# Making the 64-wide triangular inverses of chunks 0 to 11 from 16-wide blocks on VectorE and four products on TensorE

## The chip, the core and the metric

The kernel runs on one core of one Trainium2 chip. The metric is the device time of one execution in microseconds; a core has five engines that run side by side, each with its own queue in order: TensorE (PE; PEld are its weight loads), VectorE (DVE), ScalarE (ACT), GpSimd (POOL) and SyncE (SP), which here issues nearly all DMAs.

## What is computed

For 4 batches of 8 heads, 768 time steps and a head width of 40, a linear recurrence carries a 40x40 state; its outputs go through a gated network with a spatial mixing over time. Cut to what matters (all float32):

```python
for t in range(S):                       # S = 768, state [B, H, D, D], D = 40
    y[:, :, t] = einsum('bhd,bhde->bhe', r_t, state)
    Sa = einsum('bhde,bhe->bhd', state, a_t)
    state = state * w_t[:, :, None, :] - einsum('bhd,bhe->bhde', Sa, b_t) \
          + einsum('bhd,bhe->bhde', v_t, k_t)
x = y as [B, S, H * D]                   # H * D = 320
h = maximum(x @ w_in, 0)                 # d_ff = 1024
u, v = h[..., :512], h[..., 512:]
v_n = (v - mean(v)) / sqrt(var(v) + 1e-6)
out = (u * (einsum('ts,bsd->btd', w_spatial, v_n) + b_spatial[:, None])) @ w_out
```

## The kernel before

Time is cut into chunks of 64 steps. Two batches go together, so there are 24 chunks (`NS`), 12 for each pair of batches, and each chunk has 16 units (2 batches x 8 heads): 8 places in the free dimension (`NU`) times two halves of the partitions (0 to 63 and 64 to 127; `par` in the code).

Within a chunk the recurrence is turned into matrix products. The dependence of a step on the steps before it is a strictly lower triangular 64x64 matrix L for each unit, and the inverse of (1 + L), transposed, is needed as the tile `xf`. A chunk runs through these steps, each named as in the code:

- **Preparation** (`prep_load`, `prep_piece`, `scan1`, `scan2`, `at_mul`, `sl_mul`): VectorE scans the decays and multiplies the keys with them. It runs four or more chunks ahead. `lprime` and `lblock` make the two 32x32 diagonal blocks of each unit's L and put them, masked with `maskl`, into `Lc`, in which four chunks (a group, `GS`) come together.
- **Inversion** (`invert`): VectorE transposes a group's `Lc` so that every partition holds one 32x32 block, runs 30 pairs of multiply (into the PSUM tile `itmp`) and add (into `A`) over growing and shrinking rectangles, and transposes the result back twice, once straight (`XT0`) and once transposed (`X11`). Group 0 is inverted in one go before chunk 0; the steps of the others are spread between the work of earlier chunks.
- **Assembly** of the 64-wide inverse: `b_l21` multiplies out the off-diagonal 32x32 block, `b_zt` and `b_x21` multiply it with the two diagonal inverses on TensorE; ScalarE evicts (`b_l21_out`, `b_zt_out`, `b_x21_out`) and copies the diagonal blocks into `xf` (`b_xcopy`).
- **Other work ahead of the chain:** `b_copy` (a DMA into `At`), `b_lka` and `b_h` (products that ScalarE evicts and GpSimd's `strict` masks), `b_tok` (transposes).
- **The chain from chunk to chunk:** `c_bp` (products with the state `Mc`), `c_ff`, `c_xx` (products with `xf`), `c_mp` and `c_mp_out` (the new `Mc`), `c_y` and `c_y_out` (the outputs, a multiply on VectorE, line 654), `y_store`.
- **The dense network** from chunk 11 on, between the chunks: `m_load`, `m_split`, `m_u`, `m_v`, `m_n1` to `m_n3`. Its weights are decoded on VectorE and ScalarE (`decode64_steps`) during chunks 4 to 9. The spatial mixing and the last product follow in `phase2`.

The order of all this is written out by hand. `at(t, fn, ...)` puts a step into a plan at the time t, counted in chunks ("slot 3" is t from 3 to 4); the plan is sorted and issued in that order, so it sets every engine's queue. The times in a chunk's slot come from dictionaries:

```python
REG = dict(copy=0.11, lka=0.115, lka_out=0.17, tok=0.40, ..., x=0.50, x21=0.78, x21_out=0.81, dt=0.03)
LEAD = dict(REG, zt=0.88, zt_out=0.90, x=0.975, x21=1.12, x21_out=1.16)
```

The assembly for chunk q stands in slot q-1 (`REG`); that of a group's first chunk reaches into slot q (`LEAD`), as does that of chunk 1 (`FIRST`). All the small products before the chain (`lprime`, `b_lka`, `b_tok`, `b_h` and the assembly) share the two PSUM buffers named `bk`.

Of the kernel before, what the change touches and what calls it, by code (L numbers as in the profile page):

```python
# [217 lines left out]
def phase1(ctx, tc, early, late, vtok, win, xs, vns, uts, dscr):  # L218
# [125 lines left out]
    def lblock(s):  # L344
        if s % GS == 0:
            st["Lc", s // GS] = inv.tile([P, GS * NU, HB], F32, name="Lc")
        Lc = st["Lc", s // GS]
# [1 line left out]
        nc.vector.tensor_tensor(
            out=Lc[:, u0:u0 + NU, :], in0=st.pop(("pl", s)),  # L350
            in1=maskl.unsqueeze(1).broadcast_to([P, NU, HB]), op=ALU.mult,
        )

    def invert(g):
        Lc = st.pop(("Lc", g))
        A = inv.tile([P, HB, HB], F32, name="A")
        nc.vector.transpose(out=A, in_=Lc.rearrange("p u t -> p t u"))
        yield
        nc.vector.memset(A.rearrange("p t s -> p (t s)")[:, 0:HB * HB:HB + 1], 1.0)
        for k in range(1, HB - 1):  # L360
            m = HB - 1 - k
# [1 line left out]
            nc.vector.tensor_tensor(  # L363
                out=tp, in0=A[:, k + 1:, k:k + 1].broadcast_to([P, m, k]),
                in1=A[:, k:k + 1, 0:k].broadcast_to([P, m, k]), op=ALU.mult,
            )
# [5 lines left out]
        nc.vector.transpose(out=XT0.rearrange("p u t -> p t u"), in_=A)  # L372
        yield
        nc.vector.transpose(out=X11.rearrange("p u t -> p t u"), in_=A.rearrange("p t s -> p s t"))
        yield

    INV_N = HB + 1
# [33 lines left out]
    def b_lka_out(s, par):  # L411
# [3 lines left out]
        if s in LKA_POOL:  # L415
            nc.scalar.activation(At[par][ev], pk[ev], AF.Copy)  # L416
# [18 lines left out]
    def b_h_out(s, par):  # L435
        ev = PR[1 - par]
        Rt = Rts[s % 2]
        if s in H_POOL:
            nc.scalar.activation(Rt[par][ev, :, 0:C], st["ph", s][ev], AF.Copy)
# [84 lines left out]


# [60 lines left out]
    def c_xx_out(s, g):  # L586
# [3 lines left out]
        if s in TRI_POOL:  # L590
            for par in range(2):
                done = nc.scalar.activation(Rt[par][PR[par], gp], xx[PR[1 - par]], AF.Copy, scale=-1.0)  # L592
            marks["a", s] = done.ins
            for par in range(2):
                strict(Rt[par][PR[par], gp, 0:C], NP)
            return
        for par in range(2):
            nc.scalar.activation(Rt[par][PR[par], gp, C:], xx[PR[1 - par], :, C:], AF.Copy, scale=-1.0)
        for par in range(2):
            ur, ev = PR[par], PR[1 - par]  # L600
            nc.vector.tensor_tensor(
                out=Rt[par][ur, gp, 0:C], in0=xx[ev, :, 0:C],
                in1=maskn[ev].unsqueeze(1).broadcast_to([64, NP, C]), op=ALU.mult,
            )
# [421 lines left out]
```

## Time and profile before

| | |
|---|---|
| median of 3 runs | 669.57 us (663.91 to 670.55) |
| profiled execution | 665.08 us, span 663.3 us, mean granted clock 0.943 |
| PE busy | 571.8 us (86%) |
| PEld busy | 518.3 us (78%) |
| DVE busy | 448.4 us (68%) |
| ACT busy | 384.2 us (58%) |
| POOL busy | 225.9 us (34%) |

The span is the profiled execution from its first to its last instruction; its time has 1.8 us around that. Busy times are sums over the span, and engines lead in different parts of it. PEclk is the clock that TensorE was granted, as a share of full speed; a product takes longer at a lower one. In rows of instructions "128x30" is partitions x elements, "64\*64 64x104" is the weight tile and the moving tile, and "x32" counts records; one float32 product of these sizes leaves two. Releasers behind "<-" say what an engine waited for.

### The profile page before, as it was taken

The page shows a single profiled execution, that of the slowest core. Times are in us where ns is not written, and L with a number is a line of the kernel's source. Part 1 is how long each engine was busy: PE and PEld are TensorE (multiplying, and loading weights), DVE is VectorE, ACT ScalarE, POOL GpSimd, SP SyncE. Part 2 cuts the span into 40 slices and gives each one's busy share as a digit, 9 for nine tenths or more (in the row PEclk, how much of TensorE's full clock was granted, in tenths as well). Part 3 has the DMA queues.
Part 4 walks back from the last instruction along what each step waited for, and adds up shares of the span by engine and source line. Part 5 has one row for each costly group of instructions (what it writes and reads, how often), then busy time and mean ns, then how long its engine had stood idle before and what let it go on. Part 6 is the DMA issues. An engine that isn't in the chain of part 4 may idle for free.

```text
span 663.3 us, 25848 instructions
## 1 busy us (share of the span) xinstructions
PE 571.8 (86%) x10960; PEld 518.3 (78%) x10960; DVE 448.4 (68%) x970; ACT 384.2 (58%) x860; POOL 225.9 (34%) x298
## 2 busy tenths in 40 slices
PE   1447885498777887999999999999989999999997
PEld 1437674487766776888888888888878999999997
DVE  8999789989999999488896677343384842332220
ACT  2135662377666775688878887888765543221212
POOL 6013330224332334144341332332354843352221
PEclk9967997789787898999999999999998999999999
DMA  8654778477555546657565365375395557150001
GB/s 199 121 107 67 134 152 147 70 175 155 135 127 115 131 117 120 142 127 172 154 190 148 86 173 144 90 198 132 89 262 182 162 155 240 61 157 31 31 31 59
DMA packets 106331, 87.68 MB, mean 132 GB/s; under 512 B 35496, under 2 KB 92072, under 8 KB 104296
## 3 DMA queue, kind: packets, MB, share of 16 engines
q1 hardware_dynamic: 105672, 84.31, 52.0%
q10 hardware_dynamic: 544, 1.72, 1.2%
q8 instruction: 86, 1.41, 1.0%
q14 instruction: 29, 0.24, 0.1%
HBM read 59.20 MB, written 20.50 MB: 120 GB/s over the span
## 4 chain that ended last, share of the span: by engine, by line
PE 63%; DVE 15%; DMA 7%; issue 6%; ACT 4%; SPq 3%; POOL 1%; DVEq 0%; ACTq 0%; POOLq 0%
PE po L199 6%; PE pv L759 6%; PE pv L712 6%; PE pg L179 5%; PE pg L180 5%; PE pg L181 5%; PE ch L563 4%; PE bp L545 4%; PE ch L581 4%; PE bk L429 2%; DMA ein<-in_early 2%; DVE itmp L363 2%; PE bk L451 2%; PE bk L399 2%; PE bp L641 2%
## 5 line engine op out<-in xcount | busy, mean ns | idle before, releaser
L406 POOL TENSOR_SCALAR_AFFINE_SELECT Rt<-Rt 64x512 f32<-64x512 f32 (+1 forms) x144 | 83.8, 584 | 156.2 <-ACT Rt L592 128.5
L406 POOL TENSOR_SCALAR_AFFINE_SELECT At<-At 64x512 f32<-64x512 f32 x48 | 41.5, 864 | 164.0 <-ACT At L416 151.9
L555 ACT ACTIVATE Rt<-bp 64x416 f32<-64x416 f32 x96 | 49.1, 511 | 56.2 <-PE bp L545 53.6
L363 DVE TENSOR_TENSOR itmp<-A 128x30 f32<-128x30 f32 (+9 forms) x180 | 66.5, 369 | 3.4
L179 PE MATMUL pg<-wsh,vh 128*128 128x384 f32 x192 | 65.4, 341 | 2.0 <-ACT vh L51 2.0
L545 PE MATMUL bp<-lin,Mc 40*64 40x104 f32 x768 | 47.3, 278 | 22.1 <-DVE y L654 19.8
L183 DVE TENSOR_TENSOR g<-pg,bb 128x384 f32<-128x384 f32 x32 | 17.8, 556 | 70.7 <-PE pg L181 68.4
L180 PE MATMUL pg<-wsl,vh 128*128 128x384 f32 x192 | 65.1, 339 | 0.0
L181 PE MATMUL pg<-wsh,vl 128*128 128x384 f32 x192 | 63.6, 339 | 0.0
L367 DVE TENSOR_TENSOR A<-A,itmp 128x30 f32<-128x30 f32 (+9 forms) x180 | 59.1, 328 | 6.2
L545 PEld LDWEIGHTS bp<-lin,Mc 40*64 40x64 f32 x768 | 40.7, 150 | 25.5 <-DVE y L654 22.7
L563 PE MATMUL ch<-Rt,At 128*64 128x104 f32 x768 | 48.0, 283 | 5.9 <-issue 4.8
L55 POOL TENSOR_TENSOR gl<-g,gh 128x384 fp32r<-128x384 f32 x32 | 33.0, 1035 | 58.1 <-ACT gh L51 58.1
L592 ACT ACTIVATE Rt<-ch 64x416 f32<-64x416 f32 x96 | 49.1, 511 | 4.6 <-PE ch L581 2.2
L563 PEld LDWEIGHTS ch<-Rt,At 128*64 128x64 f32 x768 | 42.2, 157 | 10.4 <-issue 7.1
L51 ACT ACTIVATE gh<-g 128x384 fp32r<-128x384 f32 x32 | 16.7, 521 | 54.3 <-DVE g L184 54.3
L339 PE MATMUL bk<-at,sl 64*32 64x32 f32 x1536 | 21.2, 203 | 26.5 <-DVE sl L324 20.7
L55 POOL TENSOR_TENSOR vl<-raw,vh 128x512 fp32r<-128x512 f32 x24 | 31.5, 1324 | 31.6 <-ACT vh L51 30.1
L581 PE MATMUL ch<-ffs,xf 64*64 64x104 f32 x768 | 41.7, 261 | 0.0
L339 PEld LDWEIGHTS bk<-at,sl 64*32 64x32 f32 x1536 | 17.7, 114 | 29.5 <-issue 14.4
L179 PEld LDWEIGHTS pg<-wsh,vh 128*128 128x128 f32 x192 | 36.6, 190 | 2.4 <-ACT vh L51 2.2
L630 DVE TENSOR_TENSOR Mc<-ch,scn 104x160 f32<-104x160 f32 x44 | 18.5, 436 | 29.0 <-PE ch L619 18.7
(132 smaller groups left out, 1497.8 us busy)
## 6 DMA issues: line engine op xcount, KB each, us to landing
ein<-in_early SPq DMA_DIRECT2D x108, 129.0 KB
lin<-in_late SPq DMA_DIRECT2D x48, 160.0 KB
At<-at SPq DMA_DIRECT2D x48, 128.0 KB
...
```

Of the source, the lines that this page charges most:

```text
L55: eng.tensor_tensor(out=lo, in0=x, in1=hi.bitcast(F32), op=ALU.subtract)
L179: nc.tensor.matmul(pg, lhsT=vh[:, dc], rhs=w_h, start=(i == 0), stop=False)
L180: nc.tensor.matmul(pg, lhsT=vh[:, dc], rhs=w_l, start=False, stop=False)
L181: nc.tensor.matmul(pg, lhsT=vl[:, dc], rhs=w_h, start=False, stop=(i == NT - 1))
L363: nc.vector.tensor_tensor(out=tp, in0=A[:, k + 1:, k:k + 1].broadcast_to([P, m, k]), in1=A[:, k:k + 1, 0:k].broadcast_to([P, m, k]), op=AL ...
L367: nc.vector.tensor_tensor(out=A[:, k + 1:, 0:k], in0=A[:, k + 1:, 0:k], in1=tp, op=ALU.add)
L406: nc.gpsimd.affine_select(out=t, in_=t, pattern=[[0, k], [1, C]], base=0, channel_multiplier=-1, compare_op=ALU.is_gt, fill=0.0,)
L545: nc.tensor.matmul(bp[PR[par], q, :], lhsT=Mc[RR[par], n, :], rhs=li[RR[par], n, C:], start=(q == 0), stop=False, skip_group_check=True,)
L555: nc.scalar.activation(Rt[par][PR[par], gp, :], st["bp", g][PR[par]], AF.Copy)
L563: nc.tensor.matmul(ff[PR[1 - par], q, :], lhsT=At[par][:, n, :], rhs=Rt[par][:, n, :], start=True, stop=True,)
L581: nc.tensor.matmul(xx[ev, q, :], lhsT=xf[ev, n, :], rhs=ffs[ev, q, :], start=True, stop=True,)
L592: done = nc.scalar.activation(Rt[par][PR[par], gp], xx[PR[1 - par]], AF.Copy, scale=-1.0)
```

## The change

For groups 0, 1 and 2 (`INV16`), that is chunks 0 to 11, VectorE inverts only the four 16x16 diagonal blocks of each unit, two at a time in one instruction, in 14 pairs of steps instead of 30. The mask `maskl` gets a second version that keeps the 16-wide blocks. X11 comes before XT0 in these groups.

TensorE then makes the 64-wide inverse. With D the block-diagonal inverse and N the part of L outside the 16-wide blocks, `b_no` multiplies out L and `b_no_out` evicts the columns outside the blocks in three ScalarE instructions with a mask column of `cm` as scale (into `noT`); `b_diag` spreads the inverted blocks over a 64-wide tile, twice (D and its transpose), by two multiplies on GpSimd each (on ScalarE for the first D of chunk 0); `b_k1` multiplies N with D and ScalarE evicts K1; `b_y1`, `b_y2` and `b_y3` multiply K1 with what is there, the first and the third result are added to `xf` on VectorE, the second is evicted by ScalarE. Each of these products is 64x64x64 for each of the 16 units. They take the place of `b_l21`, `b_zt` and `b_x21`; groups 3, 4 and 5 keep these.

Around it, `maskp` and `maskn` go with the branches that used them (which no chunk took), `l21` and `zt` share buffers with the new tiles, the plan gets new times, the loads and scans of some chunks, the decoding and the first loads and splits of the dense network move by less than half a slot, and every third `vr` of the dense network lies in `noT`.

```diff
+    INV16 = {0, 1, 2}
+    ADD1, ADD3, DACT = (), (), {0}
+    S0 = (0.4, 0.401, 0.402, 0.4005, 0.405, 0.406, 0.41, 0.411, 0.415, 0.416)
+    SREG = {'no': 0.28, 'no_out': 0.285, 'd0': 0.23, 'k1': 0.36, 'k1_out': 0.365, 'd1': 0.24, 'y1': 0.66, 'y1_out': 0.665, 'y2': 0.8, 'y2_out': 0.805, 'y3': 0.98, 'y3_out': 0.985}
+    SLEAD = {'no': 0.44, 'no_out': 0.445, 'd0': 0.88, 'k1': 0.9, 'k1_out': 0.905, 'd1': 0.89, 'y1': 1.02, 'y1_out': 1.025, 'y2': 1.1, 'y2_out': 1.105, 'y3': 1.22, 'y3_out': 1.225}
+    SFIRST = {'no': 0.407, 'no_out': 0.408, 'd0': 0.43, 'k1': 0.85, 'k1_out': 0.855, 'd1': 0.44, 'y1': 1.06, 'y1_out': 1.065, 'y2': 1.12, 'y2_out': 1.125, 'y3': 1.2, 'y3_out': 1.205}
...
     def invert(g):
+        wide = g in INV16
+        W = SB if wide else HB
+        nb = HB // W
...
-        for k in range(1, HB - 1):
-            m = HB - 1 - k
-            tp = ps_i.tile([P, m, k], F32, name="itmp")
+        for k in range(1, W - 1):
+            m = W - 1 - k
+            tp = ps_i.tile([P, nb, m, k], F32, name="itmp")
             nc.vector.tensor_tensor(
-                out=tp, in0=A[:, k + 1:, k:k + 1].broadcast_to([P, m, k]),
-                in1=A[:, k:k + 1, 0:k].broadcast_to([P, m, k]), op=ALU.mult,
+                out=tp, in0=B[:, :, k + 1:W, k:k + 1].broadcast_to([P, nb, m, k]),
+                in1=B[:, :, k:k + 1, 0:k].broadcast_to([P, nb, m, k]), op=ALU.mult,
             )
...
+    def b_no(s):
+        Et, at, sl = st["pre", s]
+        m1 = ps_k.tile([P, NU, C], F32, name="bk")
+        for n in range(NU):
+            for par in range(2):
+                nc.tensor.matmul(
+                    m1[PR[1 - par], n, :], lhsT=sl[PR[par], n, par, :], rhs=at[PR[par], n, :],
+                    start=True, stop=True,
+                )
+    def b_no_out(s):
+        for j in range(1, C // SB):
+            cs = slice(j * SB, (j + 1) * SB)
+            nc.scalar.activation(noT[:, :, cs], m1[:, :, cs], AF.Copy, scale=cm[:, j - 1:j])
+    def b_diag(s, k):
+        out = xfs[s % 2] if k else st["D", s]
+        for h in range(2):
+            dst, src, m = out[:, :, h * HB:(h + 1) * HB], st["X", s // GS][1 - k][:, u0:u0 + NU], cm[:, 3 + h:4 + h]
+            if s in DACT and not k:
+                nc.scalar.activation(dst, src, AF.Copy, scale=m)
+            else:
+                nc.gpsimd.tensor_scalar(out=dst, in0=src, scalar1=m, scalar2=None, op0=ALU.mult)
+    def blocks(s, lhsT, rhs, add=None):
+        ps = ps_k.tile([P, NU, C], F32, name="bk")
+        for n in range(NU):
+            for ev in PR:
+                nc.tensor.matmul(ps[ev, n, :], lhsT=lhsT[ev, n, :], rhs=rhs[ev, n, :], ...)
+        return ps
+    def b_k1(s):      st["ps", s] = blocks(s, noT, st["D", s])
+    def b_k1_out(s):  nc.scalar.activation(k1, st["ps", s], AF.Copy)
+    def b_y1(s):      st["ps", s] = blocks(s, st["K1", s], xf, ...)
+    def b_y2(s):      st["ps", s] = blocks(s, st["K1", s], xfs[s % 2])
+    def b_y2_out(s):  nc.scalar.activation(y2, st["ps", s], AF.Copy)
+    def b_y3(s):      st["ps", s] = blocks(s, st["K1", s], st["D", s], ...)
+    def b_add(s, on_pe):                       # y1_out and y3_out
+        nc.vector.tensor_tensor(out=xf, in0=st["ps", s], in1=xf, op=ALU.add)
...
-    SCR, SLM = {4: 0.68}, {5: 0.83}
-    PREP = {4: 0.03, 5: 0.45, 6: 1.03, 7: 1.45, 8: 2.03, 9: 2.45, 10: 3.03, 11: 3.45}
+    PREP = {4: 0.207, 5: 0.53, 6: 1.03, 7: 1.41, 8: 2.03, 9: 2.45, 10: 2.88, 11: 3.45, 14: 6.05, 12: 3.93}
+    LPQ = {5: 1.15, 6: 0.78, 13: 0.78, 4: 1.05}
+    INV_T = {1: (2.5, 3.7), 2: (4.5, 7.4)}
+    OV = {(scr_store, 4): 0.68, (sl_mul, 5): 1.13, (scan2, 4): 0.4075, (at_mul, 4): 0.497, (sl_mul, 4): 0.507, (scan2, 5): 0.96, (at_mul, 5): 0.97, (scan1, 11): 3.61}
...
-    T_DEC, T_MOE = 4.2, 11
+    T_DEC, DSP, T_MOE = 4.03, 0.953, 11
...
-        at(max(own[0] - 1.6, 2 * j + 2.1, T_DEC + 5.92), m_load, bq, i)
-        at(max(own[0] - 0.45, 2 * j + 2.7), m_split, bq, i)
+        at(max(own[0] - 1.6, 2 * j + 2.1, T_DEC + 5 * DSP + 7 * 0.1 + 0.02), m_load, bq, i)
+        at(max(own[0] - 0.6, 2 * j + 2.7), m_split, bq, i)
```

The twelve times of a series' steps (`no` to `y3_out`) are those of `SREG`, `SLEAD` (first chunks of groups 1 and 2), `SFIRST` (chunk 1) and `S0` (chunk 0).

More of the change, by code (lines that the diff above doesn't have):

```diff
@@ L371, in invert, with inv_n @@
         st["X", g] = (XT0, X11)
[L372 to L377, printed above, removed]
+        outs = [(XT0, A), (X11, A.rearrange("p t s -> p s t"))]
+        for x, a in outs[::-1] if wide else outs:
+            nc.vector.transpose(out=x.rearrange("p u t -> p t u"), in_=a)
+            yield
+    def inv_n(g):
+        return (SB if g in INV16 else HB) + 1
     def lin_load(s, par):
@@ new lines, in blocks @@
+    def blocks(s, lhsT, rhs, add=None):
+        ps = ps_k.tile([P, NU, C], F32, name="bk")
+        if add is not None:
+            nc.tensor.matmul(ps, lhsT=ident, rhs=add, start=True, stop=False, skip_group_check=True)
+        for n in range(NU):
+            for ev in PR:
+                nc.tensor.matmul(
+                    ps[ev, n, :], lhsT=lhsT[ev, n, :], rhs=rhs[ev, n, :], start=add is None, stop=True,
+                    skip_group_check=add is not None,
+                )
+        return ps
@@ L589, in c_xx_out @@
         xx = st["xx", g]
[L590 to L596, printed above, removed]
         for par in range(2):
-            nc.scalar.activation(Rt[par][PR[par], gp, C:], xx[PR[1 - par], :, C:], AF.Copy, scale=-1.0)
+            done = nc.scalar.activation(Rt[par][PR[par], gp], xx[PR[1 - par]], AF.Copy, scale=-1.0)
+        marks["a", s] = done.ins
         for par in range(2):
[L600 to L604, printed above, removed]
+            strict(Rt[par][PR[par], gp, 0:C], NP)
     def c_mp(s, g):
@@ L812, in phase1 @@
         at(T["lka"], b_lka, q)
+        at(T["h"], b_h, q)
+        if q // GS in INV16:
+            S = SFIRST if q == 1 else SREG if q % GS else SLEAD
+            series(q, {k: q - 1 + t for k, t in S.items()})
+            continue
         at(T["l21"], b_l21, q)
@@ L894, in phase1 @@
             p.affine_select(
-                out=maskl[rows], in_=maskl[rows], pattern=[[1, HB]], base=0,
+                out=maskl[rows], in_=maskl[rows], pattern=[[0, 2], [1, HB]], base=0,
                 channel_multiplier=-1, compare_op=ALU.is_gt, fill=0.0,
+            )
+            p.affine_select(
+                out=maskl[rows, 1, SB:], in_=maskl[rows, 1, SB:], pattern=[[0, SB]], base=1 - SB,
+                channel_multiplier=1, compare_op=ALU.is_gt, fill=0.0,
             )
@@ L905, in phase1 @@
         make_identity(nc, ident)
-        for m, val in ((maskp, 1.0), (maskn, -1.0)):
-            p.memset(m, val)
-            for rows in PR:
-                p.affine_select(
-                    out=m[rows], in_=m[rows], pattern=[[1, C]], base=0,
-                    channel_multiplier=-1, compare_op=ALU.is_gt, fill=0.0,
-                )
+        p.memset(cm, 1.0)
+        p.memset(cm[:, 0:3], -1.0)
+        for rows in PR:
+            p.affine_select(
+                out=cm[rows, 0:3], in_=cm[rows, 0:3], pattern=[[SB, 3]], base=SB,
+                channel_multiplier=-1, compare_op=ALU.is_gt, fill=0.0,
+            )
+            p.memset(cm[rows.start:rows.start + HB, 4:5], 0.0)
+            p.memset(cm[rows.start + HB:rows.stop, 3:4], 0.0)
+        p.memset(noT[:, :, 0:SB], 0.0)
         for t in (Mc, *xfs):
@@ L944, in phase1 @@
             b_tok_out(0, par)
[L945 to L946 removed]
+        if 0 in INV16:
+            b_no(0)
+            b_no_out(0)
+        else:
+            b_l21(0)
+            b_l21_out(0)
         b_h(0)
```

143 lines of the change are left out of this document (87 added, 56 removed).

## The prediction

> **What bounds the kernel now.** I began with the page: how the five engines stand and how that changes over the span.
>
> ```profile
> PE 571.8 (86%) x10960; PEld 518.3 (78%) x10960; DVE 448.4 (68%) x970; ACT 384.2 (58%) x860; POOL 225.9 (34%) x298
> ...
> PE   1447885498777887999999999999989999999997
> ...
> DVE  8999789989999999488896677343384842332220
> ```
>
> TensorE (PE) has the most work, but a slice is 16.6 us, and up to the 16th (some 265 us) VectorE (DVE) shows 7 to 9 while PE shows 1 to 9; from there PE stands at 9. So there are two kernels in one: VectorE leads up to chunk 11, TensorE from there to the end, and the edit trades work of the first for work of the second just where the roles change. The trade has to be made stage by stage. The last of a chunk's y multiplies (line 654) marks its end; that of chunk 11 is shown, and I cut the busy time of the engines at the ends of chunks 0, 1, 3, 7, 9 and 11.
>
> ```profile
> 277.38 0.42 DVE L654 TENSOR_TENSOR y<-bp,Et 104x256 f32<-104x256 f32 x1 [0.78 <-PE bp L641]
> core 0: us, PE busy (x) PEld busy (x) DVE busy (x) ACT busy (x) POOL busy (x), PEclk, DMA share, GB/s
> ...
> 26.00:54.10 28.10, 14.09 (x259) 12.84 (x258) 25.95 (x65) 10.57 (x24) 4.17 (x6) 0.67 0.41 77
> 54.10:65.30 11.20, 10.46 (x302) 9.09 (x301) 10.32 (x15) 7.88 (x20) 6.34 (x6) 0.77 0.56 85
> 65.30:82.30 17.00, 14.03 (x443) 12.06 (x431) 12.10 (x17) 11.48 (x27) 6.27 (x9) 1.00 0.78 137
> 82.30:134.20 51.90, 31.66 (x952) 27.79 (x954) 47.88 (x97) 22.55 (x52) 11.90 (x16) 0.84 0.66 121
> 134.20:206.90 72.70, 58.47 (x1680) 51.50 (x1677) 67.87 (x134) 49.99 (x113) 23.77 (x32) 0.90 0.64 143
> 206.90:241.80 34.90, 30.05 (x824) 26.84 (x826) 33.89 (x69) 25.00 (x57) 10.36 (x16) 0.86 0.55 122
> 241.80:277.80 36.00, 30.61 (x743) 27.00 (x740) 26.95 (x53) 23.43 (x53) 12.37 (x18) 0.91 0.64 134
> 277.80:475.10 197.30, 196.12 (x4364) 170.20 (x4353) 127.85 (x333) 161.47 (x367) 67.77 (x104) 1.00 0.53 143
> ```
>
> In the rows from 82.3 to 241.8 VectorE works 149.6 of 159.5 us. In the row from 65.3 to 82.3 it does not lead; there one chunk costs PE 14.0 us at the full granted clock (1.00), the yardstick for a chunk without the edit. In the last row PE is busy 196.1 of 197.3 us: when PE is the bound, this program leaves it hardly any idle time. Nothing of the edit works there, so I carry every microsecond won before 277.8 to the end unchanged.
>
> **The removed work.** The first inversion stands alone on VectorE:
>
> ```profile
> 26.02 1.94 DVE L357 STREAM_TRANSPOSE A<-Lc 128x1024 f32<-128x1024 f32 x1
> 28.03 0.20 DVE L363 TENSOR_TENSOR itmp<-A 128x30 f32<-128x30 f32 x1
> ...
> 30.20 0.40 DVE L363 TENSOR_TENSOR itmp<-A 128x130 f32<-128x130 f32 x1
> ...
> 52.17 1.97 DVE L374 STREAM_TRANSPOSE X<-A 128x1024 f32<-128x1024 f32 x1
> 56.42 3.04 PE L581 MATMUL ch<-ffs,xf 64*64 64x104 f32 x32
> 82.30:134.20 51.90, 25.86 (x64) 0.84 0.66 121
> 134.20:206.90 72.70, 27.68 (x64) 0.90 0.64 143
> ```
>
> (The xx products of chunk 0 start at 56.4; the last two rows count only what touches the tile A: inversions 1 and 2, 25.9 and 27.7 us.) Thirty pairs and three transposes take 26.02 to 54.1, 28.1 us. The 14 new pairs have 28 to 112 elements; four old pairs of 30 to 108 elements take 28.03 to 30.20, 0.54 us each. So 14 x 0.56 = 7.9 us, with three transposes of 1.9 in all 13.6: **about 14 us less per inversion**, 42 us for three. The second block in the access pattern has no row. I bound it by nothing and by 0.1 us an instruction (130 elements took 0.40 once, twice the 0.20 of 30), 2.8 us an inversion, and take nothing: the cost follows the count of elements.
>
> **The added work.** Prices come from the nearest rows:
>
> ```profile
> 67.99 1.15 PE L399 MATMUL bk<-at,sl 64*64 64x64 f32 x32 [0.84 <-ACT Rt L555]
> 69.07 1.65 PE L563 MATMUL ch<-Rt,At 128*64 128x104 f32 x32
> ...
> 80.07 0.69 PE L514 MATMUL bk<-zt,X 32*32 32x32 f32 x32
> 80.69 1.09 PE L641 MATMUL bp<-Rt,tk 128*40 128x64 f32 x32
> L183 DVE TENSOR_TENSOR g<-pg,bb 128x384 f32<-128x384 f32 x32 | 17.8, 556 | 70.7 <-PE pg L181 68.4 <-POOL gl L55 2.3
> L349 DVE TENSOR_TENSOR Lc<-bk,maskl 128x256 f32<-128x256 f32 x24 | 10.1, 419 | 5.5 <-PE bk L339 5.5
> L406 POOL TENSOR_SCALAR_AFFINE_SELECT Rt<-Rt 64x256 f32<-64x256 f32 x96 | 50.0, 521 | 137.2 <-ACT Rt L592 128.5 <-PE ch L581 2.4 <-POOL Rt L406 0.4
> L439 ACT ACTIVATE Rt<-bk 64x512 f32<-64x512 f32 x48 | 28.0, 584 | 2.3 <-PE bk L429 1.6
> L776 ACT ACTIVATE xf<-XT 128x256 f32<-128x256 f32 x24 | 9.9, 413 | 11.6 <-DVE XT L372 11.4
> ```
>
> - **TensorE (PE):** sixteen 64x64 products (32 records) take from 67.99 to the next start at 69.07, 1.08 us; sixteen 32-wide ones 80.07 to 80.69, 0.62. A chunk gets five for three: 5.4 - 1.9 = **+3.5 us**, 42 us over 12 chunks. VectorE's 42 us come back as PE time; the gain is only what PE can take in its gaps.
> - **VectorE:** two adds of 128x512 from PSUM per chunk. By the slope of 0.42 us (256 elements) to 0.56 (384), 0.69 each: **+1.4 us** a chunk.
> - **ScalarE:** nine small copies go, three of 128x128 and two of 128x512 (0.58) come: a little less work on an engine with room.
> - **GpSimd:** four multiplies of 128x256 a chunk have no row; between 0.4 (ScalarE's copy of that size) and twice the 64x256 select, 1.0; I take 0.5, as that select. 2 us a chunk beside 6.3 in a slot of 17: hidden unless rival B holds.
>
> At one place the Trainium skill speaks otherwise. TensorEngine Tiling (Array Packing), section Instruction Overhead, has about 60 cycles for any small matmul, so 32 and 64 columns would cost about the same; the rows above (0.62 against 1.08 us) disagree. By that rule the extra of a chunk would be two products of 0.62, 1.2 us, and the sum that of rival A.
>
> **The sum, stage by stage,** against the profiled execution's own 665.08 us:
>
> 1. Start. Inversion 0 gives X11 at about 37.7 instead of XT at 52.2: -14.5. Then chunk 0's series stands on the path alone: diagonals (0.8 on ScalarE), k1, y1, y2, y3 at 1.1 each, two evictions of 0.6, two adds of 0.7, and the second transpose and a product of chunk 1 in between: about 9.6 us to the xx products, for the 4.2 from 52.2 to 56.4 now. **-9.** PE's granted clock there is 0.67; were it half, four products cost 4 us more: -5 to -10.
> 2. Rest of slot 0: the clock is 0.77 now and PE stays busier: **-1** (-2 to +2).
> 3. Slot 1 gets y1 to y3 of chunk 1 and the whole series of chunk 2: 14.0 - 1.9 + 8 x 1.08 = 20.8 of PE in a slot of 17.0: **+3.8** (0 to +5).
> 4. Slots 2 and 3: VectorE 47.9 - 12.2 + 1.4 = 37.1, and its present idle time of 4.0 on top, 41.1 for 51.9: **-10.8** (-6 to -13). PE, 31.7 + 4.5, stays below.
> 5. Slots 4 to 7: VectorE 67.9 - 14 + 5.4 = 59.3 and 4.8 idle, 64.1; but PE needs 4 x 14.0 + 4 x 3.5 + 1 (the lead of chunk 8) = 71. PE is late next: 71.2 for 72.7, **-1.5** (-7 to +3).
> 6. Slots 8 and 9 hold inversion 3, still 32 wide, and adds of three chunks: VectorE 33.9 + 4.1 - 2 (the decoding moves ahead) + 1.0 idle = 37; PE 28 + 10.5 = 38.5. For 34.9: **+3.6** (0 to +5).
> 7. Slots 10 and 11: PE 30.6 + 3.5 = 34.1 in 36.0. **0** (-4 to +3).
>
> Sum: -9 - 1 + 3.8 - 10.8 - 1.5 + 3.6 = **-15 us**, 650 us. Three runs gave 663.91 to 670.55, median 669.57; the profiled one is at their low end, and from the median I would come to 654.6. I say **651**.
>
> The moved steps I cost at nothing. The scans of chunks 4 and 5 go back by a tenth to a third of a slot, and with them the loads behind them on SP's queue (six pieces each for chunks 6 and 7, the scr stores); cover is the rest of a slot before inversion 1 at 2.5 needs chunk 7, and gone it costs some of term 4, as the DMA share is 0.78 in slot 1. The first x loads go from 10.12 to 9.62, ahead of chunk 10's scn load and At copies on SP, and wait for the last decoding step on VectorE; if that is late, Mc of chunk 10 waits: 0 to 3 us, in term 7's range. On GpSimd, four more selects stand ahead of the pads of chunks 2 and 3, whose scans stand behind those of chunks 0 and 1 anyway. The third vr buffer works behind 277.8, where PE hardly waits.
>
> **Rivals.**
>
> A. PE has room: waits that PE has now shorten with VectorE's queue, and products fall into the holes.
>
> ```profile
> PEld bp L545 <- DVE y L654: 22.7, 17, 4.6
> PE bp L545 <- DVE y L654: 19.8, 11, 4.5
> ```
>
> These 42.5 us are PE waiting for the end of a chunk on VectorE. If 28 of them go, two thirds, the products cost 1.2 us a chunk net: slot 1 gains nothing and loses nothing, slots 4 to 7 fall to VectorE's 64 (-8.6), slots 8 and 9 to +2: -9 - 1 - 10.8 - 8.6 + 2 = -27, **638**. Against it: the yardstick of 14.0 is already without such waits. Chance 0.17.
>
> B. GpSimd's multiplies hold VectorE up.
>
> ```profile
> 86.89 2.04 POOL L406 TENSOR_SCALAR_AFFINE_SELECT At<-At 64x512 f32<-64x512 f32 x2 [4.94 <-ACT At L416]
> 56.81 0.69 DVE L318 TENSOR_TENSOR at<-ein,Et 128x512 f32<-128x512 f32 x1
> 87.45 0.96 DVE L318 TENSOR_TENSOR at<-ein,Et 128x512 f32<-128x512 f32 x1
> ```
>
> The same multiply takes 0.69 with GpSimd idle and 0.96 beside its selects: 0.27 lost. If each of the four multiplies held VectorE for its whole 0.5 us, 2 us a chunk: slots 2 and 3 +4, slots 4 to 7 +1 (VectorE 72 over PE's 71), slots 8 and 9 +2.5 (41 over 38.5), so -7, **658**. Chance 0.12. (The Trainium skill, SBUF — State Buffer, section Who interferes with whom, has a two-input VectorE instruction wait until the GpSimd instruction ends; by this row the loss is a part of it.)
>
> C. Slower: PE, in order, waits for the adds. y2 cannot start before y1's add has come through VectorE's queue, and the two PSUM buffers of the products come free with the adds. The 28 waits of rival A average 1.5 us; 18 such waits (two for each of the nine chunks of the PE-bound slots) make +27, so +12, **677**. It decides from 0.8 us a wait. Against: the plan puts h (1.08 us, a product of the size priced above) and the mp products between y1 and y2, and VectorE's queue gets shorter. Chance 0.06.
>
> D. The change doesn't do what it says: VectorE's steps do not shrink with their elements. The pairs would have to cost 1.0 us for that; the rows exclude it (0.54). Chance 0.01.
>
> **How the numbers follow.** Forecast (-8 to -21) 0.6, A 0.17, B 0.12, C 0.06, D 0.01, the rest for what I have not named. Range 634 (A and a little) to 665 (B, with the runs' own spread of 6 us). A measurement of this kernel cannot tell less than about 1%, 6.7 us, from no change. Faster by over 1%: 0.82; within 1%: 0.11; slower: 0.07.
>
> **What would show it.** X11 at 37 to 39 us and the first xx at 46 to 51; inversions 1 and 2 at 13 to 14 us of VectorE each; slot 1 longer than 17 us; chunk 3's end near 117; PE at 9 tenths from slot 4, not from chunk 11; chunk 11's end at 260 to 265 and the same 197 us from there to chunk 22. The prediction fails if PE idles on the adds (more rows "PE bk <- DVE xf" than 1 us a chunk), if loads come late in slots 0 to 3, or if moved SBUF addresses give phase 2 another tile to wait for.

## The result: slower, and the profile after

The changed kernel takes 696.46 us (median of 4 runs, 695.54 to 700.24) beside 667.81 for the kernel before on the same chip (4 runs): a ratio of 1.044, interval 1.037 to 1.052. The prediction was 651. Its profiled execution has a span of 694.5 us, 31.2 more than the 663.3 before. The medians given here and below are over all executions of a kernel; the ratios leave out the few of them (at most three) that fell into a slower state.

The page after, with the engines' totals and three of the rows of 40 slices (17.4 us each):

```profile
PE 606.8 (87%) x11728; PEld 550.2 (79%) x11728; DVE 432.6 (62%) x898; ACT 371.5 (53%) x814; POOL 280.4 (40%) x351
...
PE   1478886786797877999999999999997998999997
...
DVE  8967688666777886888978567543374630532221
...
POOL 5046452546425554432442332333244313874221
```

Up to the 16th slice VectorE has come down from 8 and 9 to mostly 6 to 8, as forecast. But TensorE stands at 6 to 9 from the third slice on, not at 9: in these slices **no engine is full**. GpSimd has gone from 225.9 to 280.4 us. The stages, cut as in the prediction at the ends of chunks 0, 1, 3, 7, 9, 11 and 22 of this execution (the last of a chunk's y multiplies, now line 720):

```profile
299.22 0.42 DVE L720 TENSOR_TENSOR y<-bp,Et 104x256 f32<-104x256 f32 x1 [0.76 <-PE bp L707]
core 0: us, PE busy (x) PEld busy (x) DVE busy (x) ACT busy (x) POOL busy (x), PEclk, DMA share, GB/s
57.90:83.00 25.10, 21.41 (x668) 19.21 (x666) 17.29 (x24) 11.03 (x24) 12.96 (x12) 0.93 0.78 135
83.00:127.60 44.60, 32.44 (x950) 28.33 (x946) 39.15 (x68) 19.54 (x44) 19.45 (x23) 0.91 0.63 123
127.60:214.80 87.20, 69.45 (x1856) 63.00 (x1856) 61.63 (x109) 45.17 (x95) 41.15 (x48) 0.91 0.57 118
214.80:260.10 45.30, 38.30 (x1088) 34.49 (x1088) 36.98 (x74) 23.32 (x50) 23.10 (x27) 0.92 0.47 106
260.10:299.60 39.50, 35.10 (x864) 31.68 (x851) 28.94 (x56) 22.39 (x49) 17.12 (x22) 0.91 0.50 112
299.60:499.30 199.70, 197.19 (x4368) 170.44 (x4355) 133.85 (x333) 161.72 (x367) 67.68 (x104) 1.00 0.52 141
```

Slots 4 to 7 take 87.2 us, with PE busy for 69.5 and VectorE for 61.6. PE's is below the 71 of the prediction, VectorE's 2 us above its 59.3, and the stage is 16 us longer than the 71. So the loss is idle time on PE. The chain of waits in the stretch from 57.9 to 299.6 us names what ended it (us in all, times, longest):

```profile
POOL At L424 <- ACT At L433: 55.2, 8, 8.2
...
PEld bk L567 <- POOL ma L559: 30.3, 10, 5.5
PE bk L567 <- POOL ma L559: 28.4, 10, 5.3
```

Line 567 is the block product, and with ma the first of them, k1; ma is the tile D, the scaled copy of the inverse's diagonal blocks that GpSimd makes on line 559. Ten of these products wait 2.8 us each on average (PEld's row is the same waits seen from the weight loads, not more of them). The timelines of GpSimd, ScalarE and PE in slot 5 show one of them:

```profile
158.24 2.58 POOL L424 TENSOR_SCALAR_AFFINE_SELECT At<-At 64x512 f32<-64x512 f32 x2 [7.25 <-ACT At L433]
160.81 3.36 POOL L559 TENSOR_SCALAR ma<-X,cm 128x256 f32<-128x256 f32 x2
...
157.59 1.19 ACT L433 ACTIVATE At<-bk 64x512 f32<-64x512 f32 x2
158.69 0.85 ACT L547 ACTIVATE noT<-bk,cm 128x128 f32<-128x128 f32 x3
...
157.26 1.65 PE L639 MATMUL ch<-Rt,At 128*64 128x104 f32 x32
164.23 1.97 PE L567 MATMUL bk<-ma,noT 64*64 64x64 f32 x32 [5.33 <-POOL ma L559]
```

GpSimd sits idle for 7.25 us, because next in its queue stand the selects of At, and At is still being made by PE and ScalarE. When At comes, the two selects run (2.58), then the two multiplies (3.36). k1's other operand, noT, is there at 159.54. PE, in order, stands for 5.33 us. The inverse that the multiplies read had been there since 120.5, and the tile ma was free once the chunk before had its y3, at 154.10: GpSimd could have made D in the last 4.1 of its own 7.25 idle us.

The prices of the new operations on GpSimd and VectorE (shapes kept apart; mean ns behind the busy us):

```profile
L559 POOL TENSOR_SCALAR ma<-X,cm 128x256 f32<-128x256 f32 x22 | 32.7, 1493 | 3.2 <-PE bk L567 3.2
L567 PE MATMUL bk<-ma,noT 64*64 64x64 f32 x384 | 18.7, 268 | 29.8 <-POOL ma L559 28.4 <-ACT ma L557 1.4
L559 POOL TENSOR_SCALAR xf<-XT,cm 128x256 f32<-128x256 f32 x24 | 25.3, 1062 | 0.0
L593 DVE TENSOR_TENSOR xf<-bk,xf 128x512 f32<-128x512 f32 x24 | 16.5, 689 | 35.0 <-PE bk L567 27.4 <-POOL Rt L424 7.6
L567 PE MATMUL bk<-ma,mb 64*64 64x64 f32 x384 | 14.1, 221 | 2.3 <-ACT ma L600 1.5 <-issue 0.7
```

A multiply takes 1.06 to 1.49 us, not 0.5. VectorE's add takes the 0.69 of the prediction to the last digit. k1 costs 268 ns a record where y3 costs 221. The k1 of 164.23 ran at a granted clock of 0.50:

```profile
164.23:166.20 1.97, 1.97 (x33) 1.85 (x34) 0.50 (x3) 0.00 (x0) 1.83 (x2) 0.50 0.83 139
```

So did the five others that had waited 2.3 us or more, with 1.97 us each; the six that had waited 1.6 us or less ran at 1.00 and took 1.15. A wait of PE cost more than its own length here.

### The profile page after: what moved, and what is told of

Read it like the earlier page. It is cut to its first block, busy times and chain, and to the rows that moved or that the text cites. A ratio compares the mean times of both kernels' runs of the same rounds, so it can differ in the third digit from the quotient of the medians.

```text
span 694.5 us, 27319 instructions
## 1 busy us (share of the span) xinstructions
PE 606.8 (87%) x11728; PEld 550.2 (79%) x11728; DVE 432.6 (62%) x898; ACT 371.5 (53%) x814; POOL 280.4 (40%) x351
## 4 chain that ended last, share of the span: by engine, by line
PE 50%; DMA 5%; ACT 5%; DVE 4%; issue 2%; POOL 2%; SPq 1%; ACTq 0%; POOLq 0%
PE po L200 5%; PE pv L778 5%; PE pg L180 5%; PE pg L181 5%; PE pg L182 4%; PE pv L829 4%; PE ch L657 3%; PE bp L621 2%; PE ch L639 2%; PE bk L567 2%; PE bk L457 2%; PE bk L417 1%; PE bp L707 1%; PE bk L441 1%; PE ch L685 1%
## 5 line engine op out<-in xcount | busy, mean ns | idle before, releaser
L424 POOL TENSOR_SCALAR_AFFINE_SELECT Rt<-Rt 64x512 f32<-64x512 f32 (+1 forms) x144 | 80.6, 561 | 125.8 <-ACT Rt L667 96.2
L182 PE MATMUL pg<-wsh,vl 128*128 128x384 f32 x192 | 61.5, 340 | 0.0
L378 DVE TENSOR_TENSOR itmp<-A 128x108 f32<-128x108 f32 (+15 forms) x132 | 45.4, 344 | 2.1
L567 PE MATMUL bk<-ma,noT 64*64 64x64 f32 x384 | 18.7, 268 | 29.8 <-POOL ma L559 28.4
L621 PE MATMUL bp<-lin,Mc 40*64 40x104 f32 x768 | 41.6, 255 | 2.1 <-issue 1.5
L382 DVE TENSOR_TENSOR A<-A,itmp 128x108 f32<-128x108 f32 (+15 forms) x132 | 39.6, 300 | 4.5
L567 PEld LDWEIGHTS bk<-ma,noT 64*64 64x64 f32 x384 | 16.8, 177 | 32.0 <-POOL ma L559 30.3
L639 PE MATMUL ch<-Rt,At 128*64 128x104 f32 x768 | 41.1, 256 | 0.2
L657 PEld LDWEIGHTS ch<-ffs,xf 64*64 64x64 f32 x768 | 37.4, 141 | 3.2 <-issue 1.7
L621 PEld LDWEIGHTS bp<-lin,Mc 40*64 40x64 f32 x768 | 36.2, 136 | 4.4 <-issue 2.2
```

Of the source, the lines that this page charges most:

```text
L182: nc.tensor.matmul(pg, lhsT=vl[:, dc], rhs=w_h, start=False, stop=(i == NT - 1))
L378: nc.vector.tensor_tensor(out=tp, in0=B[:, :, k + 1:W, k:k + 1].broadcast_to([P, nb, m, k]), in1=B[:, :, k:k + 1, 0:k].broadcast_to([P, nb ...
L424: nc.gpsimd.affine_select(out=t, in_=t, pattern=[[0, k], [1, C]], base=0, channel_multiplier=-1, compare_op=ALU.is_gt, fill=0.0,)
L567: nc.tensor.matmul(ps[ev, n, :], lhsT=lhsT[ev, n, :], rhs=rhs[ev, n, :], start=add is None, stop=True, skip_group_check=add is not None,)
L621: nc.tensor.matmul(bp[PR[par], q, :], lhsT=Mc[RR[par], n, :], rhs=li[RR[par], n, C:], start=(q == 0), stop=False, skip_group_check=True,)
L639: nc.tensor.matmul(ff[PR[1 - par], q, :], lhsT=At[par][:, n, :], rhs=Rt[par][:, n, :], start=True, stop=True,)
```

## The experiments

All ratios are to the kernel before, run beside the changed one. The first four runs ask two things: is the wait for D the loss, and is it GpSimd's place in the order, its time, or its work beside VectorE; and what does the rest of the change do by itself.

**No 16-wide group: the rest alone.**

```diff
-    INV16 = {0, 1, 2}
+    INV16 = set()
```

> No group is inverted the new way (INV16 empty); what is left of the change are its moved steps, the third vr buffer in noT and the moved addresses. Theory T (TensorE stands at the first product of the series, k1, until GpSimd has spread D; 10 waits and 29.8 us of idle PE in the changed kernel, and a lower clock behind them): the series is gone and with it most of the loss, 665 to 677 us; the 9 us that the changed kernel loses behind chunk 11 (5 up to chunk 23, 4 in phase 2) may stay. Rival R1 (the five products are too much work for PE, wherever D comes from): the same, 665 to 677. Rival R2 (the moved steps or the moved addresses are the loss): 690 or more.

674.59 us (672.18 to 676.46), ratio 1.011 [1.005, 1.017]: rival R2 falls, while T and R1 both gave this range. The moved steps, the third vr buffer and the moved addresses cost 1% where no series is there to use the room. In slot 1 (26.4 us, for 16.9) a moved scan stands in VectorE's queue before its load has landed, and PE waits behind it for Lc (waits from 65.4 to 91.8 us):

```profile
DVE S L299 <- DMA ein<-in_early: 7.0, 1, 7.0
...
PE bk L520 <- DVE Lc L356: 4.7, 1, 4.7
```

That is a loss of this mixture only: in the changed kernel VectorE waits 2.5 us for a load in slot 1. What both share is the part behind chunk 11: 393.7 us here, 394.9 after, 385.5 before.

**D on ScalarE for all twelve chunks.**

```diff
-    ADD1, ADD3, DACT = (), (), {0}
+    ADD1, ADD3, DACT = (), (), set(range(12))
```

> The changed kernel with the first spreading (D for k1) of all twelve chunks on ScalarE, as chunk 0 has it, in place of GpSimd; the second one stays on GpSimd. T: the waits of PE on D go (29.8 us) and the clock behind them stays up, 655 to 668 us. R1: PE is busy anyway, 690 or more. R2: 690 or more.

674.29 us (674.04 to 676.9), ratio 1.012 [1.007, 1.017]: span 672.3, **22.2 us won back** by moving 22 copies to another queue. The copy takes 498 ns there, and no row of k1 waiting for POOL is left. R1 (690 or more) falls; theory T had the waits right, but its 655 to 668 was 6 us too low. Its groups, and its stages from the end of chunk 0 to that of chunk 11 with their sum:

```profile
L567 PE MATMUL bk<-ma,noT 64*64 64x64 f32 x384 | 14.0, 221 | 5.2 <-ACT noT L547 3.0 <-ACT ma L557 2.2
L557 ACT ACTIVATE ma<-X,cm 128x256 f32<-128x256 f32 x24 | 10.8, 498 | 1.8 <-PE bk L567 1.3 <-DVE X L391 0.4
...
57.60:80.50 22.90, 20.39 (x670) 18.12 (x668) 16.73 (x24) 11.96 (x26) 11.07 (x10) 1.00 0.78 142
80.50:124.30 43.80, 33.67 (x989) 29.95 (x986) 38.19 (x68) 21.75 (x49) 16.61 (x20) 0.92 0.68 131
124.30:203.70 79.40, 66.54 (x1832) 59.54 (x1829) 62.58 (x110) 47.92 (x102) 32.31 (x39) 0.94 0.65 134
203.70:243.30 39.60, 35.63 (x1090) 31.80 (x1086) 36.97 (x74) 25.09 (x54) 18.46 (x22) 1.00 0.43 102
243.30:277.70 34.40, 32.73 (x844) 29.27 (x843) 28.57 (x56) 23.16 (x51) 16.18 (x20) 1.00 0.64 138
sum 220.10, PE 188.95 PEld 168.68 DVE 183.04 ACT 129.88 POOL 94.63; mean PE 37.79 PEld 33.74 DVE 36.61 ACT 25.98 POOL 18.93
```

**D on GpSimd still, but a quarter of a slot earlier,** ahead of the selects of At. To make that possible D has a tile of its own, and one vr buffer pays for it.

```diff
-            st["D", s] = jat.tile([P, NU, C], F32, name="ma", bufs=1)
+            st["D", s] = jat.tile([P, NU, C], F32, name="md", bufs=1)
-    SREG = {..., 'd0': 0.23, 'k1': 0.36, ...}
+    SREG = {..., 'd0': -0.02, 'k1': 0.36, ...}
-        if st["nv"] % 3 == 2:
+        if st["nv"] % 2 == 1:
-            vr = st["act"].tile([P, DH], F32, name="vr", bufs=2)
+            vr = st["act"].tile([P, DH], F32, name="vr", bufs=1)
```

> The first spreading stays on GpSimd but gets a tile of its own and is planned a quarter of a slot earlier (-0.02 in place of 0.23) for all chunks that aren't the first of a group or chunk 1, so that it stands before the At masks in GpSimd's queue and is done when PE comes to k1. To make room the dense network's vr has two buffers again, one of them noT. T with the place as the cause: as the run with D on ScalarE, 655 to 670. If it is GpSimd's time itself (four multiplies of 1.1 to 1.5 us a chunk that hold up the masks and VectorE): 675 to 690. R1 and R2: 690 or more.

675.89 us (671.82 to 677.74), ratio 1.013 [1.007, 1.018]: the time is that of D on ScalarE, but by the ranges set it falls to the rival that it is GpSimd's time. GpSimd still needs 1.15 us for each of the same 22 multiplies, and PE hardly waits for them. The last two rows are from the end of chunk 0 to that of chunk 11, and from the end of chunk 23 on:

```profile
L559 POOL TENSOR_SCALAR md<-X,cm 128x256 f32<-128x256 f32 x22 | 25.0, 1147 | 1.5 <-PE bk L567 1.5
...
PE bk L567 <- POOL md L559: 3.9, 2, 2.1
...
55.80:282.20 226.40, 195.34 (x5412) 175.17 (x5409) 182.95 (x328) 121.64 (x262) 111.61 (x129) 0.92 0.61 126
503.30:674.90 171.60, 165.06 (x1004) 161.70 (x1002) 55.94 (x133) 55.63 (x117) 66.73 (x58) 1.00 0.37 112
```

So a better **place in the order** is enough to take the waits away, with D still on GpSimd: 3.9 us of 28.4 are left. It is not the whole of the 22 us. The stretch takes 226.4 us, between the 241.7 of the changed kernel and the 220.1 with D on ScalarE; the total is level with the latter because the part behind chunk 23 is 6 us shorter (171.6 for 177.8), as in all kernels with one vr buffer fewer. Whether the 6 us that remain in the stretch are GpSimd's time is open. Nor does the run show that the duration was harmless at the old place. There, two multiplies of 0.5 us, as predicted, in place of 1.49 would have made each of the ten waits 2 us shorter; by their lengths (0.9 to 5.3 us) some 11 of the 28.4 us would have been left, by my estimate.

**None of the scaled copies on GpSimd.**

```diff
-            if s in DACT and not k:
+            if True:
```

> Both spreadings of all twelve chunks on ScalarE; GpSimd has no step of the series. T: within 3 us of the run with only D on ScalarE. If GpSimd's multiplies also cost by holding VectorE or its own masks: 5 us or more faster than that. If ScalarE's four copies a chunk (some 1.8 us) make it the bound: slower than it. R1: 690 or more.

676.73 us (674.06 to 682.29), ratio 1.016 [1.009, 1.023]. Taking the other 24 multiplies (those of xf) away from GpSimd wins nothing. From the end of chunk 0 to that of chunk 11 VectorE is busy for 179.6 us beside 183.0 with D alone on ScalarE: in these two executions the multiplies of xf took some 0.3 us a chunk from VectorE, not rival B's 0.5 us each, and with 7.6 us more on ScalarE the whole is no shorter. At its price rival B falls.

The next four runs start from D on ScalarE and ask where the remaining 1% and the predicted gain are.

**Only two vr buffers, as before.**

```diff
-        if st["nv"] % 3 == 2:
+        if False:
```

> The run with D on ScalarE (674.3 us), and the dense network's vr in its own two buffers only, none in noT. From the end of chunk 11 to the end of the program that run takes 394.6 us and the kernel before 385.5. Theory V (the third vr, which shifts the stores of v and the loads of phase 2 that wait for them, is the 9 us): 664 to 668. Theory M (the splits that come 0.15 slot earlier, ahead of the masks on GpSimd): 672 to 677. Theory A (the moved SBUF addresses, whatever vr does): 672 to 677.

668.73 us (663.81 to 675.98, 10 runs), ratio 1.006 [1.002, 1.010]. By the medians some 0.6% better than with the third buffer, but the intervals overlap, and the time lies just above theory V's range and below that of M and A. The traces are clearer. From the end of chunk 23 to the end of the program the five kernels with the two buffers and noT as the third take 177.6 to 178.7 us, all the others 171.6 to 174.2 (173.3 before). PE's waits there, after and in this kernel, each with its row of that stretch:

```profile
516.90:694.50 177.60, 167.18 (x999) 163.86 (x997) 60.35 (x135) 56.16 (x117) 68.21 (x59) 0.98 0.37 114
...
PE pg L180 <- ACT vh L52: 6.2, 2, 3.5
```

```profile
495.10:669.30 174.20, 166.24 (x1005) 163.39 (x1003) 63.34 (x135) 55.63 (x117) 66.85 (x59) 0.98 0.38 117
...
PE pg L180 <- ACT vh L52: 3.1, 1, 3.1
```

With the third buffer PE waits 3.1 us more for vh, in the gating stage. Why a deeper buffer brings this about I did not settle.

**And the splits of x where they were.**

```diff
-        at(max(own[0] - 0.6, 2 * j + 2.7), m_split, bq, i)
+        at(max(own[0] - 0.45, 2 * j + 2.7), m_split, bq, i)
```

> As the run without the third vr, and the splits of the dense network at their old time (0.45 slot ahead of the first product in place of 0.6). V: as that run, 664 to 668. M: 664 to 668 here and 672 or more there. A: 672 to 677 in both.

667.03 us (661.42 to 673.06), ratio 1.007 [1.003, 1.011]: no different from the run above by the medians. Its profile has 387.9 us behind chunk 11 for 391.3, but runs of one kernel differ by more than that.

**16-wide blocks in groups 0 and 1 only;** group 2 (chunks 8 to 11) goes back to the 32-wide inversion.

```diff
-    INV16 = {0, 1, 2}
+    INV16 = {0, 1}
-    INV_T = {1: (2.5, 3.7), 2: (4.5, 7.4)}
+    INV_T = {1: (2.5, 3.7), 2: (4.5, 7.7)}
```

> As the run with the old tail (D on ScalarE, two vr, splits at the old time), but only groups 0 and 1, chunks 0 to 7, are inverted the new way, and inversion 2 is spread to 7.7 as before. With D on ScalarE chunk 3 ended 9.9 us ahead of the kernel before, chunk 7 only 3.2 and chunk 11 not at all. Theory P (from slot 4 on PE is the bound, and the series costs there what the shorter inversion gives): the lead of chunk 3 is kept in part, 4 to 8 us ahead of the kernel before at chunk 11; 656 to 664 if the tail is as before, 665 to 672 if it is not. Theory W (the series itself is slow only through waits of its own steps): no better than with three groups.

659.15 us (657.8 to 663.15), ratio **0.995 [0.992, 0.998]**, as theory P gave; chunk 11 ends 7.9 us ahead of the kernel before. Group 2's new form alone cost 1.2%. Its series put work on PE in slots 8 to 11, where PE was busy for 60.7 of 70.9 us before the change: in the profiles these slots take 63.9 us here and 73.5 in the run above. The 14 us that it saves on VectorE lie in slots 4 to 7, which take 84.4 and 76.2. So the two stages nearly cancel in these two executions; but that of the run above is the fastest of its kernel (661.4, 5.6 us under its median), and the 1.2% rest on the medians, not on the stages.

**Two products less.** The series ends after its second term; y2, y3, their eviction and their add are left out, so the inverse is incomplete.

```diff
-           ("d1", b_diag, 1), ("y1", b_y1), ("y1_out", b_add, ADD1), ("y2", b_y2), ("y2_out", b_y2_out),
-           ("y3", b_y3), ("y3_out", b_add, ADD3))
+           ("d1", b_diag, 1), ("y1", b_y1), ("y1_out", b_add, ADD1))
```

> The run with D on ScalarE, with the products y2 and y3, the eviction of y2 and the second add left out (the inverse is then cut off after its second term). This takes 2 x 1.08 us of PE, one 0.69 us add of VectorE and one 0.6 us eviction of ScalarE from each of chunks 0 to 11. P (PE is the bound in the slots of the series): chunk 11 ends 18 to 25 us earlier than at 277.7. If VectorE or waits elsewhere are the bound: 5 to 12 us earlier (0.7 us a chunk of VectorE and 2 to 4 us at the start).

654.2 us (one run), 20 us less than with them (18 when each is taken beside its own runs of the kernel before); chunk 11 ends at 258.2, 19.5 us earlier. The sum of its stages from chunk 0 to chunk 11:

```profile
sum 201.10, PE 167.75 PEld 148.80 DVE 173.78 ACT 122.74 POOL 96.27; mean PE 33.55 PEld 29.76 DVE 34.76 ACT 24.55 POOL 19.25
```

PE is busy 21.2 us less and the stretch is 19.0 us shorter, nine tenths of that; PE's idle time stays (33.4 us for 31.2). That is what theory P said: once D is out of the way, PE's work sets the pace. It is one execution on each side, and with the products went 9.3 us of VectorE, 7.1 us of ScalarE and the waits between the steps, which this run does not tell apart from PE's work.

The last four runs ask what each group is worth, and whether the moved steps matter.

**Group 0 alone.** From the kernel of groups 0 and 1:

```diff
-    INV16 = {0, 1}
+    INV16 = {0}
```

> Only group 0 (chunks 0 to 3) has 16-wide blocks; groups 1 and 2 are inverted 32-wide; first scaled copy on ScalarE, loads of the layer behind as before. Theory S (a group pays by its stage: PE busy plus PE idle): chunk 0 ends near 56 (-9 to -10), slot 1 takes 22 to 23 (+6), slots 2 and 3 carry the 32-wide inversion 1 and two or three series with their adds, 51 to 55 (0 to +3); chunk 3 ends at 131 to 135 for 134.2, and the whole is 0.995 to 1.003 of before. Theory M (the moved scans and decoding steps are what costs, the groups themselves gain): slower than before by the some 1% that the rest alone cost, 1.005 to 1.01.

663.51 us (657.14 to 669.05), ratio 0.996 [0.992, 1.000]. The 1.005 to 1.01 of the theory that the moved steps cost is excluded. Its one profile is of its longest execution (669.05 us; chunk 0 ends at 62.3 there, for the 56 expected), so I read no stages from it.

**Group 1 alone, with the plan of before.**

```diff
-    INV16 = {0, 1}
+    INV16 = {1}
-    PREP = {4: 0.207, 5: 0.53, 6: 1.03, 7: 1.41, 8: 2.03, 9: 2.45, 10: 2.88, 11: 3.45, 14: 6.05, 12: 3.93}
-    LPQ = {5: 1.15, 6: 0.78, 13: 0.78, 4: 1.05}
+    PREP = {4: 0.03, 5: 0.45, 6: 1.03, 7: 1.45, 8: 2.03, 9: 2.45, 10: 3.03, 11: 3.45}
+    LPQ = {}
-    T_DEC, DSP, T_MOE = 4.03, 0.953, 11
+    T_DEC, DSP, T_MOE = 4.2, 1.0, 11
...
```

(The order within chunk 1's slot, GAP and OV too go back to what stood before.)

> Only group 1 (chunks 4 to 7) has 16-wide blocks, and the scans, pieces, decoding steps and loads stand where they stood before. Theory S: chunk 0 at 65.4 and chunk 1 at 82.3 as before, slots 2 and 3 lose 14 us of VectorE: 42 to 45 for 51.9, chunk 3 near 126; slots 4 to 7 have 8 to 14 us more PE work at the same 10 to 14 us of idle time: 80 to 84 for 72.7; so 0 to -3 us, 0.995 to 1.0. Theory M: with no step moved, all of the gain of slots 2 and 3 stays, -6 to -9, 0.987 to 0.991, below the version of groups 0 and 1.

659.18 us (656.52 to 661.68), ratio 0.992 [0.989, 0.996]. Its stages (slots 2 and 3, 4 to 7):

```profile
82.80:123.70 40.90, 30.36 (x938) 26.14 (x924) 34.97 (x64) 21.98 (x51) 14.20 (x17) 0.92 0.77 150
123.70:204.50 80.80, 68.18 (x1940) 60.57 (x1936) 73.08 (x143) 48.57 (x104) 35.39 (x40) 0.95 0.56 130
```

11.0 us won in slots 2 and 3, where VectorE alone was nearly full; 8.1 given back in slots 4 to 7, where PE's 58.5 became 68.2. The stages went as the theory by stages says. The ratio lies between the two theories' ranges, and its slots 10 and 11 are 6 us shorter than before, which neither foresaw; that stretch took 29.8 to 35.3 us in the three other kernels in which group 1 is 16-wide and group 2 is not, so I read nothing from it.

**Groups 0 and 1, with the later steps as before, and groups 0 and 1 once more.** For the first:

```diff
-    T_DEC, DSP, T_MOE = 4.03, 0.953, 11
+    T_DEC, DSP, T_MOE = 4.2, 1.0, 11
-    PREP = {..., 10: 2.88, 11: 3.45, 14: 6.05, 12: 3.93}
+    PREP = {..., 10: 3.03, 11: 3.45}
```

(The entry of LPQ for chunk 13 and that of OV for `scan1` of chunk 11 go too.)

> Groups 0 and 1 have 16-wide blocks, and the steps from slot 3 on (scans of chunks 10 to 14, decoding of the second layer's weights, first loads) stand where they stood before. Theory M: 2 to 4 us faster than the version of groups 0 and 1 with them moved (0.995), 0.989 to 0.992. Theory S: the same within 1 us, since 386 to 387 us from the end of chunk 11 to the end of the program are already those of before (385.5).

> The version of groups 0 and 1 once more, on the chip of the three other kernels of this call: 0.992 to 0.998 of before. If gains of groups add up, its gain is that of group 0 alone plus that of group 1 alone.

659.02 us (651.17 to 659.79), ratio **0.990 [0.984, 0.995]**, and 661.87 (654.33 to 667.29), 0.992 [0.988, 0.996]. They can't be told apart, and in the profiles the stretch behind chunk 11 is the same, 385.3 and 385.2 us. Both beat the kernel before and the changed one. Whether the gains of the groups add up (0.996 times 0.992 is 0.988) lies inside the intervals too.

## Why the prediction was wrong

The stages of before, what the prediction gave them, and what they did in the profiles after and with D on ScalarE (differences to before, us):

| stage | before | predicted | after | D on ScalarE |
|---|---|---|---|---|
| to the end of chunk 0 (steps 1, 2) | 65.4 | -10 | -7.5 | -7.8 |
| slot 1 (3) | 16.9 | +3.8 | +8.2 | +6.0 |
| slots 2, 3 (4) | 51.9 | -10.8 | -7.3 | -8.1 |
| slots 4 to 7 (5) | 72.7 | -1.5 | +14.5 | +6.7 |
| slots 8, 9 (6) | 34.9 | +3.6 | +10.4 | +4.7 |
| slots 10, 11 (7) | 36.0 | 0 | +3.5 | -1.6 |
| behind chunk 11 | 385.5 | 0 | +9.4 | +9.1 |
| sum | 663.3 | -15 | +31.2 | +9.0 |

**The step that failed first is the line on GpSimd**: "2 us a chunk beside 6.3 in a slot of 17: hidden unless rival B holds". It has two errors. The size: 4 multiplies are 5.1 us by the means, not 2, and even the upper bound of 1.0 was too low; the bounds came from another kind of instruction and from another engine. At the place that D had, that size made the waits longer, by some 17 of 28.4 us by the estimate above. But with a better place they nearly vanish at 1.15 us a multiply, so the error to learn from is the other one: to have compared a sum of busy time with a slot. An instruction on an engine that is two thirds idle is late when the one ahead of it in the queue waits for something late, and here it was the selects of At, which come out of PE itself. So PE waited for GpSimd, which waited for PE. The plan shown in the change held the answer: d0 at 0.23 stands right behind lka_out at 0.17 and 0.19, with k1 at 0.36. The prediction asked what stands ahead of GpSimd's pads, and never what stands ahead of D. Cost: 22 us. From the end of chunk 0 to that of chunk 11 (241.7 us after, 220.1 with D on ScalarE) PE's busy time fell by 7.8 us, 4.7 of them k1's records at the lower clock (18.7 for 14.0), and its idle time by 13.8: of the 28.4 us of waiting, half came back as other waits.

**Rival C named the right form and the wrong engine.** PE, in order, does wait within the series, and 10 such waits of 2.8 us lie beside its 18 of 1.5. But the marker that the prediction set, PE waiting on VectorE's adds, shows 1.7 us in all with D on ScalarE.

**Rival A's 42.5 us count one thing twice.** PEld's waits for the y multiply and PE's lie in the same moments, as the weight load and its product wait for the same release; together they cover 22.7 us, and PE's own are 11 waits of 1.8 us, not 28 of 1.5. Of them, 1.4 us are left from chunk 0 to chunk 11 with D on ScalarE. So A's waits did go, but they were half of what A counted, and other waits came: its 638 did not. Nor did rival D: X11's transpose starts at 35.98 and inversions 1 and 2 take 13.8 and 13.7 us of VectorE after.

**Rival B's 0.27 us was read as a partial loss.** Of the two selects beside that multiply (87.45 to 88.41) the first ends at 87.87:

```profile
86.89 0.98 POOL L406 TENSOR_SCALAR_AFFINE_SELECT At<-At 64x512 f32<-64x512 f32 x1 [4.94 <-ACT At L416]
```

The multiply ends 0.54 us after that. All twelve of the 24 such multiplies before that took more than 0.70 us end 0.53 to 0.55 us after the select that was running when they began. So VectorE did wait for the end of GpSimd's instruction; the loss is 0.27 us because the select had only 0.42 us left.

**The second step to fail is "hardly any idle time"**, read from the stretch 277.8 to 475.1 and carried to slots 4 to 9. From the end of chunk 0 to that of chunk 11, PE was busy 164.8 of 212.5 us before (the sum of the rows shown there): 47.7 idle. The prediction added 42 us of work and took nearly all of the idle time away. With D on ScalarE, PE's busy time grew by 24.1 us, and the idle time went from 47.7 to 31.2: 24.1 - 16.5 = +7.6 us for the stretch. Step 5 is the clearest: PE is busy 66.5 us for the 71 foreseen, and the slots take 79.4 for 71.2, since 12.9 us of PE's idle time stayed, of 14.2 before. In these early chunks PE is in a chain with four other engines. PE's largest waits in this stretch with D on ScalarE:

```profile
PE bk L457 <- DVE Lc L356: 4.6, 1, 4.6
PE bk L417 <- issue: 3.8, 2, 3.5
PE bk L567 <- ACT noT L547: 3.0, 4, 1.1
...
PE bk L567 <- DVE xf L593: 1.7, 2, 1.5
```

They are many and have no common cause; of "issue" the profile shows none. The two products left out were worth nine tenths of their PE time all the same: an engine need not be full to set the pace.

**The price of the products held; the rest of PE's work shrank.** With D on ScalarE, from the end of chunk 0 to that of chunk 11, the new products are busy for 62.4 us (12.4 + 11.7 + 25.4 + 12.9), 1.18 for sixteen; the three that they replace took 23.5 before (8.2 + 8.0 + 7.3), 0.73 for sixteen. Five for three makes +3.7 us a chunk, for the +3.5 forecast. But three other groups of PE took 67.2 us before and 52.6 now (the pairs in the same order):

```profile
L563 PE MATMUL ch<-Rt,At 128*64 128x104 f32 x352 | 25.3, 304 | 5.9 <-issue 4.8 <-DMA Rt<-in_vtok 1.1
L545 PE MATMUL bp<-lin,Mc 40*64 40x104 f32 x352 | 24.4, 297 | 21.6 <-DVE y L654 19.8 <-issue 1.9
...
L399 PE MATMUL bk<-at,sl 64*64 64x64 f32 x352 | 17.5, 272 | 0.8 <-ACT Rt L555 0.8
```

```profile
L639 PE MATMUL ch<-Rt,At 128*64 128x104 f32 x352 | 20.0, 268 | 0.0
...
L621 PE MATMUL bp<-lin,Mc 40*64 40x104 f32 x350 | 18.8, 250 | 3.6 <-issue 2.2 <-DVE y L720 1.4
...
L417 PE MATMUL bk<-at,sl 64*64 64x64 f32 x352 | 13.8, 227 | 3.8 <-issue 3.8
```

These are the products at which PE had waited for the y multiply, and those next to them. The granted clock of the stretch is 0.89 before and 0.96 here, so the likely cause is the clock of the k1 above; no run separates it. The rule of the Trainium skill that was weighed there (TensorEngine Tiling (Array Packing), section Instruction Overhead; 1.2 us a chunk by it) speaks of the latency of one product, and there the trace is near it: a record takes 196 ns for 32 columns before and 221 for 64 here. The price of a chunk is set by how sixteen follow each other, and there 0.73 and 1.18 us differ.

**The third is "costed at nothing"**: the third vr buffer and the moved steps were +9 us behind chunk 11, which the prediction let pass with "PE hardly waits" there. It looked at chunks 12 to 22. Some 4.5 of the 9 arise behind chunk 23, in the row above; the rest is spread and was not split up, except that it goes (to within 2 us) when the buffer, the splits of x and group 2 are as before.

**What held:** the start (-7.5 for -10, the first xx product at 50.33 for 46 to 51), the inversions, the adds of 0.69, and the signs of steps 1 to 4 and 6. Steps 3 to 6 came out 1 to 8 us worse than forecast with D on ScalarE: of the 24 us between the -15 and the +9.0 there, 9 lie behind chunk 11 and 8 in slots 4 to 7.
